# Sends in making order, k and v packed 5 and 4, q in quarters one block earlier, and a silu moved behind a copy

## The chip, the core and the metric

The kernel runs on one core of a Trainium2 chip. A core has TensorE (PE: matmuls, with its weight loads shown apart as PEld), VectorE (DVE), ScalarE (ACT), GpSimd (POOL) and SyncE (SP), which here does nothing but issue DMAs; its queue is called SPq. They run side by side and wait for each other through semaphores. Matmuls read SBUF and write into PSUM banks; VectorE and ScalarE carry the results from there into SBUF. GpSimd works on SBUF alone.

The metric is the device time of one execution in microseconds. The kernel before takes 1059.37 us (median of 3 runs, 1058.65 to 1060.12). The profile is of one execution with a span of 1058.9 us.

## The reference

Attention without softmax, with an RMS norm, and behind it a feed-forward block with a gate:

```python
# q, k, v: (8, 8, 576, 64) float32 = batch, head, position, dim; g_norm: (64,)
kv = np.einsum('bhsd,bhse->bhde', k, v)            # k^T v, 64 x 64 for each head
out = np.einsum('bhsd,bhde->bhse', q, kv)
rms = np.sqrt(np.mean(out * out, axis=-1, keepdims=True) + 1e-06)
attn = out / rms * g_norm

x = attn.transpose(0, 2, 1, 3).reshape(4608, 512)  # tokens x model
g = x @ w_gate                                     # w_gate, w_val: 512 x 1536
silu = g * (1.0 / (1.0 + np.exp(-g)))
val = x @ w_val
result = silu * val @ w_out                        # w_out: 1536 x 512
```

## The kernel before

The 4608 tokens go in nine blocks (n = 0 to 8) of 512. The attention of block n + 1 is worked into the feed-forward of block n. A feed-forward has an *up* part (w_gate and w_val, the silu, the product) and a *down* part (w_out).

Both parts use a Winograd form of Strassen's scheme: a product of 2 x 2 blocks in seven products instead of eight. They are called P1 to P7 and run in the order 1, 5, (4, 3 of the unit before), 6, 2, 7. Several of them add up in one PSUM bank, and intermediate states are copied out, so a product may only be added to a bank once the copy of the state before is done:

```python
    CHAIN = {1: ("b", True), 6: ("b", False), 7: ("b", False), 4: ("b", False), 2: ("a", True),
             5: ("c", True), 3: ("c", False)}          # bank of each product; True: a new one
    ...
    class Up(Quad):                                    # one of six units of the up part of block 1
        def sequence(self, last):
            return [(self, 1), (self, 5), (last, 4), (last, 3), (self, 6), (self, 2), (self, 7)]

        def after2(self):
            add(nc.vector, self.s, self.ps["a"], self.s)
            nc.scalar.activation(out=self.s, in_=self.s, func=ACT.Silu)

        def after7(self):
            self.u3 = self.piece(2)
            nc.scalar.copy(out=self.u3, in_=self.ps["b"])
            add(nc.vector, self.u3, self.ps["c"], self.u3)

        def after4(self):
            g = self.piece(3)
            nc.scalar.activation(out=g, in_=self.ps["b"], func=ACT.Silu)
            mul(nc.gpsimd, self.h[:, :, HB:BLK], g, self.u3)

        def after3(self):
            add(nc.vector, self.u2, self.ps["c"], self.u2)
            mul(nc.gpsimd, self.h[:, :, 0:HB], self.s, self.u2)
            self.ffn.ended = self.ffn.h_sums(self.j, 1, nc.vector)
```

Block 0 multiplies plainly, block 1 uses one level of the scheme (class `Up`), and blocks 2 to 8 use two in the up part (class `Inner`). The second level needs sums of sums of the weights. There are too many of these for SBUF, so block 1 makes them once on VectorE (`leaf_steps`), three steps after each product, and sends them to DRAM; the blocks after it read them back as a stream of 17 chunks for each of three d, through a pool of nine tiles (`t`). The same nine tiles hold the sums of weights that GpSimd makes for the first level. Each of the six j of block 1 sends when the steps of a group are done, ordered by chunk:

```python
        def send():
            for c, ops in enumerate(CHUNKS):
                dst = stream.dram[d, c]                # one DRAM tile for each chunk
                places = [at.get(op) for op in ops]
                if len(ops) == 2 and None not in places and places[0][0] is places[1][0]:
                    (src, i), (_, k) = places
                    tc.keep_in_program_order(nc.sync.dma_start(out=dst[:, :, f], in_=src[:, i : k + 1 : k - i]))
                    continue
                for m, place in enumerate(places):
                    if place:
                        tc.keep_in_program_order(nc.sync.dma_start(out=dst[:, m, f], in_=place[0][:, place[1]]))
```

k and v are loaded by pairs of heads (four j). The 576 positions of a head are nine groups of 64: five groups lie in partitions 0 to 63 and four in 64 to 127, so a tile of 1024 columns holds one j in 640 of them, and one quarter of those is empty in the lower half. The pool `ld` has four such tiles, shared by k, v, q and, at the start, the weights:

```python
        def kv(self, js):
            ...
            for j in js:
                for c in range(KT):                    # KT = 5
                    for r in range(2 if c < KT - 1 else 1):
                        rows = slice(r * D, (r + 1) * D)
                        for u in range(2):
                            nc.tensor.matmul(          # 64 x 64, 72 of them a block
                                self.kv_ps[r][u * D : (u + 1) * D, j, :], lhsT=self.k[j][rows, u, c, :],
                                rhs=self.v[j][rows, u, c, :], start=(c == 0), stop=(c == KT - 1 - r),
                            )
```

q must be turned. Up to block 3 TensorE does it, with 16 transposes of 128 x 128 and a copy out of PSUM. From block 4 on (`TURNED = 4`) q is loaded in 32 x 32 quarters by some 32 small DMAs, so that VectorE's transpose of 32 x 32 squares does the rest. In those blocks k and v come one j at a time, in four steps within the up part, since q takes two of the four tiles; before them two j at a time, in two steps:

```python
            elif n + 1 < TURNED:
                steps = {4: third, 8: two_thirds}      # after 4 and 8 twelfths of the up part
            else:
                steps = {3 * j + 2: lambda j=j: pair(j) for j in range(NS)}
```

Of the kernel before, what the change touches and what calls it, by code (L numbers as in the profile page):

```python
# [8 lines left out]
F32 = mybir.dt.float32  # L9
# [9 lines left out]
def kernel(  # L19
# [54 lines left out]
    KT = 5  # L74
    eps = 1e-6
# [42 lines left out]
    class Words:  # L118
# [12 lines left out]
        def __init__(self, src, shape):  # L131
            self.raw = ld_pool.tile([P, 2 * BLK], U32, name="ld")
            dst = self.raw.rearrange("p (a b) -> p a b", a=shape[0])
            nc.sync.dma_start(out=dst, in_=src)
            self.shape = shape
# [48 lines left out]
    class Att:  # L184


        def __init__(self, n):
            self.n = n

            self.cut, half = divmod(n, 2)  # L190
            self.split = half * D
            self.ps, self.z = {}, None
            self.q, self.k, self.v, self.room = [], [], [], None
            self.halves = []
# [10 lines left out]
        def place_kv(self, j, i):  # L205

            n = (2 * j + i) * 2 * KT * D
            if self.n == 0:
                return self.room.rearrange("p f t -> p (f t)")[:, n:]
            if self.n == 1 and j < 2:  # L210
                return self.room[:, n:]
            return ld_pool.tile([P, 2 * BLK], F32, name="ld")

        def load_kv(self, js):
            if self.n == B:
                return
            for j in js:
                hs = slice(2 * j, 2 * j + 2)
                for i, (tiles, src) in enumerate(((self.k, k), (self.v, v))):
                    t = self.place_kv(j, i)[:, 0 : 2 * KT * D].rearrange("p (h x) -> p h x", h=2)  # L220

                    for r, s0, m in ((0, 0, KT), (1, KT * D, KT - 1)):
                        nc.sync.dma_start(  # L223
                            out=t[r * D : (r + 1) * D, :, 0 : m * D],
                            in_=src[self.n, hs, s0 : s0 + m * D].rearrange("h (p t) d -> p h (t d)", t=m),
                        )
                    tiles.append(t.rearrange("p h (t d) -> p h t d", t=KT))

        def load_quarters(self, i):


            ld = ld_pool.tile([P, 2 * BLK], F32, name="ld")
# [16 lines left out]
        def load_q(self, i):  # L249
# [5 lines left out]
            else:  # L255
                ld = ld_pool.tile([P, 2 * BLK], F32, name="ld")
# [9 lines left out]
        def kv(self, js):  # L266
# [4 lines left out]
            if js[0] == 0:  # L271
                self.kv_ps = [m_psum.tile([P, NS, D], F32, name="m") for _ in range(2)]
            for j in js:
                for c in range(KT):
                    for r in range(2 if c < KT - 1 else 1):
                        rows = slice(r * D, (r + 1) * D)
                        for u in range(2):
                            nc.tensor.matmul(  # L278
                                self.kv_ps[r][u * D : (u + 1) * D, j, :], lhsT=self.k[j][rows, u, c, :],
                                rhs=self.v[j][rows, u, c, :], start=(c == 0), stop=(c == KT - 1 - r),  # L280
                            )
            if js[-1] == NS - 1:
# [111 lines left out]
        def first(self):  # L394
            self.turn_q(0, (b_psum, c_psum))
            self.kv(range(NS))
# [40 lines left out]
    TURNED = 4  # L437
# [44 lines left out]
    class Up(Quad):  # L482
# [22 lines left out]
        def after2(self):  # L505
            add(nc.vector, self.s, self.ps["a"], self.s)
            nc.scalar.activation(out=self.s, in_=self.s, func=ACT.Silu)

        def after7(self):
            self.u3 = self.piece(2)  # L510
            nc.scalar.copy(out=self.u3, in_=self.ps["b"])
            add(nc.vector, self.u3, self.ps["c"], self.u3)
# [145 lines left out]

    CHUNKS = (
# [5 lines left out]
    class Stream:  # L665


        def __init__(self):
            self.dram = {}
            for d in range(NP // 2):  # L670
                for c in range(len(CHUNKS)):
                    self.dram[d, c] = dram.tile([P, 2, 2, P], F32, name=f"w{d}_{c}")
            self.at = {op: (c, i) for c, ops in enumerate(CHUNKS) for i, op in enumerate(ops)}
# [7 lines left out]
        def pump(self):  # L681

            while self.next and not self.held[-9]:
                n, d, c = key = self.next.pop(0)
                k = len(CHUNKS[c])
                self.tiles[key] = t_tile(key).rearrange("p l (f c) -> p l f c", f=2)
                self.uses[key] = 2 * k
                nc.sync.dma_start(out=self.tiles[key][:, 0:k], in_=self.dram[d, c][:, 0:k])
# [19 lines left out]
    def leaf_steps(j, sources, room):  # L708
# [3 lines left out]
        at = {}  # L712
        i = 0
        for t, os in sources:
# [8 lines left out]
            )  # L723
            yield lambda b11=b11, t2_=t2_, to=to: sub(nc.vector, to[:, :, 1], b11, t2_)
            for m, o in enumerate(os):
                for r, p in enumerate((4, 7, 5)):
                    at[o, p] = room, i + 3 * m + r
                if o not in RESIDENT:
                    quarters = t[:, m].rearrange("p i e c -> p (i e) c")
                    for r, p in enumerate((1, 6, 2, 3)):  # L730
                        at[o, p] = quarters, r
            i += 3 * n

        def send():
            for c, ops in enumerate(CHUNKS):
                dst = stream.dram[d, c]
                places = [at.get(op) for op in ops]
                if len(ops) == 2 and None not in places and places[0][0] is places[1][0]:
                    (src, i), (_, k) = places
                    tc.keep_in_program_order(nc.sync.dma_start(out=dst[:, :, f], in_=src[:, i : k + 1 : k - i]))  # L740
                    continue
                for m, place in enumerate(places):
                    if place:
                        tc.keep_in_program_order(nc.sync.dma_start(out=dst[:, m, f], in_=place[0][:, place[1]]))

        yield send
# [88 lines left out]
    class Ffn:  # L835
# [22 lines left out]
        def up(self, fill):  # L858
# [11 lines left out]
            for i, this in enumerate(units):  # L870
                if i + 1 < len(units):
                    units[i + 1].prepare()
                for unit, p in this.sequence(last):
                    if unit:
                        unit.multiply(p)
                        self.make(3)
# [8 lines left out]
        def down(self, nxt):  # L885
# [3 lines left out]
            for p in (1, 5, 6, 7, 2, 4, 3):  # L889
# [5 lines left out]
                self.make(12)  # L895
# [151 lines left out]
```

## Time and profile before

| What | Value |
|---|---|
| Time | 1059.37 us (1058.65 to 1060.12) |
| VectorE busy | 701.7 us (66%) |
| ScalarE busy | 234.9 us (22%) |
| GpSimd busy | 367.5 us (35%) |
| DMA | 161.87 MB, q1 at 52.1% of 16 engines |
| Reads of the stream (`t<-w`) | 336 of 256 KB, 2.9 us each to landing, and 21 of 128 KB |
| Sends (`w<-t`, `w<-r`, `w<-xi`) | 36 + 6 + 18 of 128 KB, 42 + 36 of 64 KB, 1.8 to 2.2 us each to landing |

How to read it. A group is called by its source line, engine and tiles, output first: `t<-w` reads the stream from DRAM into a t tile, and `w<-t`, `w<-r` and `w<-xi` send parts of it. Sums, differences and products are recorded by small helpers, so L110 is any sum, L111 any difference and L112 any product. L460 is a matmul of `Quad` (`Up` and the down part), L609 one of `Inner`, L278 one of k^T v and L299 a transpose of q. L507 is the silu in `after2` and L511 the copy in `after7`; L740 and L744 are the sends, L688 the reads of the stream, L223 the loads of k and v and L241 those of q in quarters. A matmul of 32-bit numbers appears as two records. An entry such as [5.23 <-ACT r L511] says how long the engine had been idle and what released it.

### The profile page before, as it was taken

To read this page: it belongs to the slowest core of one execution; us is meant where nothing else is said; L and a number is where in the kernel's file an instruction comes from. 1 tells how busy PE (TensorE), PEld (TensorE's weight loads), DVE (VectorE), ACT (ScalarE), POOL (GpSimd) and SP (SyncE) were. 2 spreads that over 40 slices of the span, in tenths; PEclk is the share of its full clock that TensorE was granted. 3 is DMA by queue.
4 is the path that set the end of the run, shared out by engine and by line. 5 is a ranking of instruction groups with operands and counts; after the bars stand their busy time and mean duration, and the time that the engine had idled before them with its cause. 6 is when DMAs were issued, how large, how long until landed. Compare 5 with 4: busy or idle time off the path is not lost.

```text
span 1058.9 us, 21788 instructions
## 1 busy us (share of the span) xinstructions
PE 1032.9 (98%) x8700; PEld 928.2 (88%) x8700; DVE 701.7 (66%) x1255; ACT 234.9 (22%) x372; POOL 367.5 (35%) x280
## 2 busy tenths in 40 slices
PE   5899999998999999999999999999999999999998
PEld 5644688876899989998999899989999899989997
DVE  2999596777656766575666756676668556855661
ACT  2666211221112211111121211221111121112110
POOL 0000453344015711563056305640455126512670
PEclk9999999998999999999999999999999999999999
DMA  9887203565568436753476347643763266226601
GB/s 239 228 265 231 57 2 109 167 167 156 174 195 235 122 90 189 227 153 86 152 224 191 88 127 226 198 93 120 218 214 89 81 204 190 61 80 195 199 31 40
DMA packets 177076, 161.87 MB, mean 153 GB/s; under 512 B 70864, under 2 KB 128080, under 8 KB 176976
## 3 DMA queue, kind: packets, MB, share of 16 engines
q1 hardware_dynamic: 176912, 160.49, 52.1%
q8 instruction: 69, 1.13, 0.4%
q14 instruction: 31, 0.25, 0.1%
q0 software_dynamic: 64, 0.00, 0.0%
HBM read 138.02 MB, written 22.41 MB: 152 GB/s over the span
## 4 chain that ended last, share of the span: by engine, by line
PE 92%; DVE 3%; DMA 2%; SPq 2%; POOL 1%; issue 0%; ACT 0%; DVEq 0%; POOLq 0%; ACTq 0%
PE b L609 25%; PE b L460 20%; PE c L609 12%; PE c L460 10%; PE a L609 6%; PE a L460 5%; PE c L912 4%; PE b L912 4%; PE m L278 2%; PE m L366 1%; PE m L319 1%; SPq L223 1%; PE b L319 1%; DMA ld<-in_moe_w_gate_dram 1%; DVE r L111 1%; DVE r L110 1%
## 5 line engine op out<-in xcount | busy, mean ns | idle before, releaser
L110 POOL TENSOR_TENSOR r<-r 128x256 f32<-128x256 f32 (+1 forms) x105 | 110.4, 1056 | 343.4 <-DVE r L110 337.7
L110 DVE TENSOR_TENSOR r<-b,r 128x512 f32<-128x512 f32 (+1 forms) x273 | 162.2, 606 | 67.1 <-PE b L609 61.9
L111 POOL TENSOR_TENSOR t<-wo 128x512 f32<-128x512 f32 x81 | 113.5, 1422 | 185.6 <-DVE wo L110 107.7
L110 DVE TENSOR_TENSOR r<-c,r 128x512 f32<-128x512 f32 (+1 forms) x179 | 108.8, 618 | 94.7 <-PE c L609 51.6
L609 PE MATMUL b<-x,t 128*128 128x128 f32 x1092 | 151.5, 276 | 0.0
L609 PEld LDWEIGHTS b<-x,t 128*128 128x128 f32 x1092 | 136.3, 192 | 1.0
L110 DVE TENSOR_TENSOR r<-a,r 128x512 f32<-128x512 f32 (+1 forms) x99 | 62.5, 631 | 81.2 <-PE a L609 51.2
L609 PE MATMUL c<-xi,t 128*128 128x128 f32 x840 | 112.1, 275 | 0.0
L112 POOL TENSOR_TENSOR h<-r 128x1024 f32<-128x1024 f32 (+1 forms) x40 | 81.4, 2052 | 84.9 <-DVE r L110 71.4
L609 PEld LDWEIGHTS c<-xi,t 128*128 128x128 f32 x840 | 102.8, 192 | 0.0
L460 PE MATMUL b<-wo,h 128*128 128x256 f32 x432 | 98.2, 380 | 0.0
L460 PE MATMUL b<-t,h 128*128 128x256 f32 x432 | 97.1, 381 | 0.0
L460 PEld LDWEIGHTS b<-wo,h 128*128 128x128 f32 x432 | 80.6, 190 | 12.0 <-DVE h L112 1.8
L460 PEld LDWEIGHTS b<-t,h 128*128 128x128 f32 x432 | 80.7, 190 | 11.1 <-issue 0.2
L623 ACT COPY r<-b 128x512 f32<-128x512 f32 x63 | 36.9, 586 | 238.0 <-PE b L609 231.2
L609 PE MATMUL b<-xi,t 128*128 128x128 f32 x588 | 79.7, 276 | 0.0
L609 PEld LDWEIGHTS b<-xi,t 128*128 128x128 f32 x588 | 72.4, 192 | 0.0
L609 PE MATMUL b<-x,wg 128*128 128x128 f32 x336 | 52.3, 278 | 0.0
L609 PE MATMUL b<-x,wv 128*128 128x128 f32 x336 | 51.6, 276 | 0.0
L460 PE MATMUL c<-t,s 128*128 128x256 f32 x216 | 48.9, 383 | 0.0
L460 PE MATMUL a<-wo,h 128*128 128x256 f32 x216 | 48.3, 379 | 0.0
L460 PE MATMUL c<-wo,h 128*128 128x256 f32 x216 | 48.1, 379 | 0.0
(130 smaller groups left out, 1623.4 us busy)
## 6 DMA issues: line engine op xcount, KB each, us to landing
t<-w SPq DMA_DIRECT2D x336, 256.0 KB, 2.9
out_dram<-r SPq DMA_DIRECT2D x17, 512.0 KB, 2.9
ld<-in_moe_w_gate_dram SPq DMA_DIRECT2D x12, 512.0 KB, 4.9
ld<-in_moe_w_val_dram SPq DMA_DIRECT2D x12, 512.0 KB, 4.9
ld<-in_moe_w_out_dram SPq DMA_DIRECT2D x12, 512.0 KB, 4.3
w<-t SPq DMA_DIRECT2D x36, 128.0 KB, 2.1
ld<-in_k_dram SPq DMA_DIRECT2D x26, 160.0 KB, 3.3
ld<-in_v_dram SPq DMA_DIRECT2D x26, 160.0 KB, 3.4
```

The costliest lines, as they stand in the source:

```text
L110: add = lambda e, o, a, b: e.tensor_tensor(out=o, in0=a, in1=b, op=OP.add)
L111: sub = lambda e, o, a, b: e.tensor_tensor(out=o, in0=a, in1=b, op=OP.subtract)
L112: mul = lambda e, o, a, b: e.tensor_tensor(out=o, in0=a, in1=b, op=OP.mult)
L223: nc.sync.dma_start(out=t[r * D : (r + 1) * D, :, 0 : m * D], in_=src[self.n, hs, s0 : s0 + m * D].rearrange("h (p t) d -> p h (t d)", t=m),)
L278: nc.tensor.matmul(self.kv_ps[r][u * D : (u + 1) * D, j, :], lhsT=self.k[j][rows, u, c, :], rhs=self.v[j][rows, u, c, :], start=(c == 0), ...
L319: nc.tensor.matmul(self.ps[i][u][p : p + D, t, j, :], lhsT=self.qt[rows, 2 * i + t, j, p : p + D], rhs=kvs[b % 3][rows, j, :], start=True, ...
L366: nc.tensor.transpose(ps[:, e, t], xt[:, t, j + e], ident)
L460: nc.tensor.matmul(banks[e][:, e], lhsT=lhsT, rhs=rhs, start=first and i == 0 and (e == 0 or banks[0] is not banks[1]), stop=i == self.ste ...
L609: nc.tensor.matmul(ps[:, i, f], lhsT=self.weight(o, p, f), rhs=self.operand(o, p), start=first and (i, f) == (0, 0), stop=True, skip_group ...
L623: nc.scalar.copy(out=dst, in_=ps)
L912: nc.tensor.matmul(t, lhsT=w[f // 2][:, i, P * (f % 2) : P * (f % 2 + 1)], rhs=x[:, i, of], start=(i == 0), stop=(i == NS - 1),)
```

## The change

It has five parts.

- The stream lies in DRAM in the order in which it is made, one tensor for each d; a send carries all that a step has made, as soon as it is there. A read then takes two places of that tensor, which lie next to each other in seven of the seventeen chunks; one chunk is a single place and nine are two places apart. Block 1 does four making steps after each product, not three.
- k and v of two j share a tile: five groups of one j and four of the next in each half, 1152 columns without a gap. All of k and v of a block takes two steps.
- q comes in quarters from block 3 on (`TURNED = 3`), and those loads are moved from the start of the down part to behind its P5.
- The silu of `after2` goes behind the copy of P7.
- The ld tiles grow from 1024 to 1152 columns.

```diff
-    TURNED = 4
+    TURNED = 3
...
         def after2(self):
             add(nc.vector, self.s, self.ps["a"], self.s)
-            nc.scalar.activation(out=self.s, in_=self.s, func=ACT.Silu)

         def after7(self):
             self.u3 = self.piece(2)
             nc.scalar.copy(out=self.u3, in_=self.ps["b"])
+            nc.scalar.activation(out=self.s, in_=self.s, func=ACT.Silu)
             add(nc.vector, self.u3, self.ps["c"], self.u3)
...
+    LEAVES = [(o, p) for o in (5, 7, 4) for p in (1, 6, 2, 3)]
+    LEAVES += [(o, p) for os in ((5,), (7,), (4,), (1, 2), (6, 3)) for o in os for p in (4, 7, 5)]
...
-                nc.sync.dma_start(out=self.tiles[key][:, 0:k], in_=self.dram[d, c][:, 0:k])
+                nc.sync.dma_start(out=self.tiles[key][:, 0:count], in_=self.dram[d][:, i : k + 1 : max(k - i, 1)])
...
+        def send(leaf, count, src):
+            at = LEAVES.index(leaf)
+            tc.keep_in_program_order(nc.sync.dma_start(out=stream.dram[d][:, at : at + count, f], in_=src))
...                                                    # in leaf_steps, after the third step of a product
+            if os[0] not in RESIDENT:
+                yield lambda t=t, o=os[0]: send((o, 1), 4, t[:, 0].rearrange("p i e c -> p (i e) c"))
             yield lambda b11=b11, t2_=t2_, to=to: sub(nc.vector, to[:, :, 1], b11, t2_)
...
+            yield lambda i=i, n=n, o=os[0]: send((o, 4), 3 * n, room[:, i : i + 3 * n])
...
-                        self.make(3)
+                        self.make(4)
...                                                    # k and v: two j (e = 0, 1) in a tile
+            for e in range(2):
+                j = 2 * g + e
                 for c in range(KT):
-                    for r in range(2 if c < KT - 1 else 1):
-                        rows = slice(r * D, (r + 1) * D)
-                        for u in range(2):
+                    for r in range(2):
+                        m = KT - (r != e)
+                        for u in range(2 if c < m else 0):
                             nc.tensor.matmul(
-                                self.kv_ps[r][u * D : (u + 1) * D, j, :], lhsT=self.k[j][rows, u, c, :],
-                                rhs=self.v[j][rows, u, c, :], start=(c == 0), stop=(c == KT - 1 - r),
+                                self.kv_ps[r][u * D : (u + 1) * D, j, :], lhsT=self.k[j, r][:, u, c, :],
+                                rhs=self.v[j, r][:, u, c, :], start=(c == 0), stop=(c == m - 1),
                             )
...                                                    # in the down part
                 self.make(12)
+                if p == 5:
+                    for i in range(2):
+                        self.loads(i)
...
-            elif n + 1 < TURNED:
-                steps = {4: third, 8: two_thirds}
-            else:
-                steps = {3 * j + 2: lambda j=j: pair(j) for j in range(NS)}
-            ffn.up(steps)
+            ffn.up({4: third, 8: two_thirds} if nxt else {})
```

## The prediction

> **What bounds the kernel now.** I read the page first (busy time by engine), then the waits of TensorE, then the windows of the single blocks, and last the timeline of the one block in which TensorE stands still.
>
> ```profile
> PE 1032.9 (98%) x8700; PEld 928.2 (88%) x8700; DVE 701.7 (66%) x1255; ACT 234.9 (22%) x372; POOL 367.5 (35%) x280
> ```
>
> TensorE is busy 1032.9 of 1058.9 us, so at most 26 us can come from idle time; more needs fewer or better packed matmuls. The windows, one for each block of 512 tokens from block 2 on, show where it is full (columns: stretch, its length, then busy time of PE, PEld, DVE, ACT, POOL, granted clock, DMA share, GB/s):
>
> ```profile
> 295.00:407.00 112.00, 112.00 (x1065) 106.45 (x1064) 71.41 (x120) 22.65 (x35) 42.71 (x32) 1.00 0.57 162
> 407.00:517.70 110.70, 110.70 (x1046) 104.59 (x1046) 71.91 (x122) 20.60 (x31) 42.94 (x32) 1.00 0.55 159
> ...
> 849.80:956.90 107.10, 107.08 (x902) 101.67 (x902) 71.27 (x121) 20.34 (x30) 42.81 (x32) 1.00 0.45 132
> ...
> 162.34:250.52 88.18, 80.64 (x498) 69.50 (x497) 64.50 (x146) 17.86 (x32) 30.91 (x23) 0.96 0.53 146
> ```
>
> Blocks 2 to 7 have no gap: there only TensorE's own work counts. The last line is the up part of block 1, the only block that makes the streamed weights: 7.54 us idle, and the clock drops to 0.96. The waits of 160 to 300 us (waiter <- waited for: us in total, times, longest) name the links:
>
> ```profile
> ACT r L507 <- DVE r L110: 32.6, 6, 7.5
> ...
> POOL t L111 <- DMA w<-t: 13.1, 5, 4.6
> ...
> DVE s L110 <- POOL h L112: 12.1, 5, 2.9
> ...
> PE b L460 <- ACT r L511: 7.5, 2, 5.2
> ```
>
> and the timeline shows the second stall as one chain:
>
> ```profile
> 234.17 0.52 SPq L740 DMA_DIRECT2D w<-t  x1
> ...
> 234.68 1.27 POOL L111 TENSOR_TENSOR t<-wo 128x512 f32<-128x512 f32 x1 [1.21 <-DMA w<-t]
> ...
> 235.90 1.27 POOL L112 TENSOR_TENSOR h<-r 128x512 f32<-128x512 f32 x1
> ...
> 237.21 0.42 DVE L110 TENSOR_TENSOR s<-h 128x256 f32<-128x256 f32 x1 [2.93 <-POOL h L112]
> ...
> 241.19 0.68 DVE L110 TENSOR_TENSOR r<-a,r 128x512 f32<-128x512 f32 x1
> ...
> 241.91 0.63 ACT L507 ACTIVATE r<-r 128x512 f32<-128x512 f32 x1 [7.47 <-DVE r L110]
> ...
> 242.45 0.57 ACT L511 COPY r<-b 128x512 f32<-128x512 f32 x1
> ...
> 243.16 3.75 PE L460 MATMUL b<-x,t 128*128 128x256 f32 x8 [5.23 <-ACT r L511]
> ...
> 246.70 2.72 PE L460 MATMUL c<-x,wv 128*128 128x256 f32 x8
> ```
>
> GpSimd cannot refill a t tile before a send of its old content is done; VectorE waits for GpSimd's product; the sum of P2 comes late; ScalarE stands at the silu of that sum, with the copy of P7 behind it; and P4 may not add into that bank before the copy. The sends lag since the DMA queue is nearly full: the program has 138 of them (36 + 42 + 36 + 18 + 6 in the DMA view), and adding up that queue's timeline from 160 to 276 us gives 81.3 us for them and 94.9 us in all: 0.59 us a send.
>
> **What the Trainium skill says.** Perfetto Trace Analysis, section What "DMA-bound" means, counts as one kind of bound a DMA sequencer whose track is solid issue slices. It fits: 94.9 of 116 us, while the 16 DMA engines are only 0.53 busy. TensorE: Matmul & The Clock Gate, section What's actually happening, says that an idle window of some 3.4 us halves the clock. The trace agrees: after the 5.23 us gap four matmuls take 3.54 us (243.16 to 246.70) instead of 1.73, and the next four 2.56; the gap of 2.31 us slows nothing. DMA: Bandwidth & Descriptors, section Specifications, puts full rate at 512 B and more. I take the measured side: from 50 to 60 us the weight loads, in runs of 1 KB, keep the engines at a share of 1.01 with 296 GB/s, while the stream in runs of 2 KB has 159 GB/s at 0.55, which is 289 at a full share. So reads in runs of 1 KB should cost what they cost now.
>
> **The change part by part.**
>
> 1. *Sends by making order.* The sends of a j go from 23 to 8 (three products with two each, two pairs with one each), 138 to 48 in all: 48 x 0.59 = 28 us of issue in place of 81. Each also leaves right after the step that makes its data, no longer after all steps of its group. With it, three steps for each product of block 1 become four: a j has 20 sums and 8 sends, 28 steps, which is 4 x 7 products, so the making keeps pace. Now it is 24 steps against 3 x 7 = 21, so a rest is done in the down part. The t tiles come free sooner, and GpSimd's wait of 13.1 us should nearly go.
>
> 2. *Silu behind the copy of P7.* The copy no longer stands behind a wait for VectorE. P4 is free as soon as P7 ends. What is left is P3, which needs VectorE's sum of P7 out of bank c, and P4 before it takes 1.73 us, so VectorE may be later by that much for nothing.
>
> Parts 1 and 2 hit the same loss: 2.31 + 5.23 = 7.54 us idle, and the cold clock after it, (3.54 - 1.73) + (2.56 - 1.73) = 2.64 us; 10.2 us together. I keep 1.5 us of it as a rest, since VectorE gets tighter: 64.5 us busy now, and the making left after 250.5 us (seven sums in the timeline, 1.69 + 1.48 + 1.01 + 1.02 = 5.2 us) moves in, 69.7 us in about 78, 89%. Gain 8.7 us.
>
> 3. *q in quarters from block 3 on.* Block 3's q is turned on TensorE in block 2. Timeline of TensorE there:
>
> ```profile
> 360.37 0.60 PE L299 MATMUL m<-ident,ld 128*128 128x128 f32 x4
> ...
> 362.11 2.11 PE L460 MATMUL b<-wo,h 128*128 128x256 f32 x9
> ```
>
> 362.11 - 360.37 = 1.74 us leave TensorE. In return VectorE makes two 128x1024 transposes of 1.23 us (as the ten that it makes for later blocks), in a block where it is busy 71 of 112 us: free. The 32 small loads take 16.6 us of the DMA queue (361.43 to 378.06, for block 4 today). They now go into the down part, ahead of the first stream reads, as they already do in later blocks. Gain 1.7 us.
>
> 4. *k and v packed, two steps.* No matmul is saved: 72 of 64x64 a block, before and after. But each switch to 64x64 and back costs time. A burst of 36 (72 records in the timeline) runs from 311.73 to 313.04; the 18 of the quartered form (36 records) run from 430.67 to 431.39. The first is 1.31 us, the second 0.72 us, so two of 18 cost 0.13 us more than one of 36 in the burst alone. Around each, the matmul before and the group after it are drawn out by 0.10 us each (0.55 between the first and second group after, otherwise 0.45). So a burst of 36 costs 1.51 and two of 18 cost 1.84. For a block, 3.68 - 3.02 = 0.66 us. A cross-check: block 2 has two bursts and the transposes, block 3 four bursts and none, and chain starts give 111.76 (295.23 to 406.99) against 110.70; 111.76 - 1.74 = 110.02, which is 0.68 under 110.70. I take 0.68, for blocks 3 to 6: gain 2.7 us.
>
> 5. *Start.* The same 16 k and v loads in block 0, but all k of a pair of j ahead of its v, so the last matmuls wait for one load more. Cost 0.3 us by judgement; the wait for the gate weights behind it covers some.
>
> Sum: 8.7 + 1.7 + 2.7 - 0.3 = 12.8 us. From 1059.37 that is 1046.6 us.
>
> **Rivals.** *VectorE takes the stall over.* If it stays as late as now (its sum of P7 starts at 243.73, though P7 ended at about 237.1), P3 would wait where P4 waited: P4 at 237.9, done at 239.7, P3 not before 244.4 (243.73 + 0.68), so only 0.5 of the 5.23 us is won, and by the same reckoning 0.9 of the 2.31. That is 1.4 us instead of 8.7: about 1054 us. Against it: VectorE's lag in that chain is waiting (2.93 us and then 1.15 us for GpSimd), not work, and what GpSimd waited for is the send. *The stream starves.* All reads come from one tensor for each d, nine of the seventeen chunks (the strided pairs) in runs of 1 KB instead of 2, and 32 q loads stand before the first reads. If 1 KB runs halved the rate, the share of 0.55 would go towards 0.85, with TensorE waiting in every block, 1065 us or more. Against it: the 296 GB/s above, the nine t tiles of lead, and the first reads, which today start 15 us before their use (276.21 against 291.56) and need to start no later relative to it. *k and v loads hold up the queue.* A load that waits for k^T v blocks the reads behind it; today that is 26.0 us in 14 waits without one gap on TensorE, and block 2, which already loads in two steps, has none either. It would cost 0 to 4 us. *Only part 2 or only part 1 works*: either alone should remove most of the second stall, so the sum changes by 2 to 4 us.
>
> **Range and chances.** The 4.4 us of parts 3 and 4 are TensorE's own work, which nothing hides; I trust them to 1 us. The block 1 term can be 4 to 11 us. That gives 1043.5 to 1051. 2% is 21.2 us: faster than 1038.2 would need nearly all of the idle time of the kernel, of which some 15 us lie in the first 40 us that the change hardly touches: 2%. Slower than 1080.6 needs the starving stream in every block: 2%.
>
> **What would show it.** Right: no TensorE wait on ScalarE's copy in block 1; a granted clock of 1.00 there and an up part of 78 to 80 us; GpSimd's wait for sends under 4 us; 48 sends; blocks 2 to 6 at 110.0 us each; two k^T v bursts per block; no idle TensorE in blocks 2 to 7. Wrong: TensorE waiting for VectorE at the P3 of block 1 (first rival), or for stream reads in blocks 2 to 8, or a DMA share well above 0.55 at the same GB/s (second rival).

## The result, and the profile after

| | Before | After |
|---|---|---|
| Time, median | 1059.6 us (1058.65 to 1060.12, 4 runs) | 1053.33 us (1053.17 to 1053.51, 4 runs) |
| Ratio | 1 | 0.9942, 95% interval 0.9925 to 0.9959 |
| Span of the profiled execution | 1058.9 us | 1051.5 us |

Predicted were 1046.6 us, and 1043.5 to 1051 as the range. The kernel gained about half of the 12.8 us.

In the kernel after, the helpers are one line further down: L111 is any sum, L112 any difference, L113 any product. L468 is a matmul of `Quad`, L518 the copy of P7, L519 the silu of the sum of P2, L726 the sends. Busy time by engine, from the page:

```profile
PE 1026.1 (98%) x8684; PEld 923.0 (88%) x8684; DVE 706.9 (67%) x1257; ACT 232.7 (22%) x368; POOL 368.7 (35%) x280
```

The windows of the kernel after: the up part of block 1, then the blocks 2, 3, 6 and 7, each from its first P1 to that of the next block (columns as before):

```profile
162.45:247.60 85.15, 80.01 (x498) 68.89 (x497) 70.69 (x148) 17.67 (x32) 30.84 (x23) 0.98 0.63 175
...
292.45:402.43 109.98, 109.96 (x1047) 104.22 (x1046) 71.71 (x122) 20.69 (x31) 42.79 (x32) 1.00 0.56 160
402.43:512.41 109.98, 109.96 (x1046) 104.23 (x1046) 71.71 (x122) 20.69 (x31) 42.80 (x32) 1.00 0.56 160
...
732.37:842.35 109.98, 109.96 (x1046) 104.22 (x1046) 71.70 (x122) 20.69 (x31) 42.80 (x32) 1.00 0.52 149
842.35:949.42 107.07, 107.05 (x902) 101.69 (x901) 71.30 (x121) 20.32 (x30) 42.80 (x32) 1.00 0.44 132
```

Blocks 2 to 6 take 109.98 us each, full to the last 0.02, as predicted. The up part of block 1 takes 85.15 us with 5.14 of them idle; predicted were 78 to 80. Laid from one down chain's first matmul to the next, the profiled executions differ by: start +0.27; block 1 129.21 to 126.18, -3.03; block 2 111.76 to 108.84, -2.92; block 3 109.65 to 109.98, +0.33; blocks 4 to 6 110.70 to 109.98, three times -0.72; block 7 +0.06. That is 7.45 us; the spans differ by 7.4, the medians by 6.0 to 6.3, so the profiled execution of before was one of its longer ones. Block 1 alone falls short.

The waits of the kernel after from 160 to 300 us show that every link of the old chain is still there (waiter <- waited for: us in total, times, longest):

```profile
POOL t L112 <- DMA w<-t: 35.8, 6, 10.0
ACT r L519 <- DVE r L111: 33.3, 6, 7.5
...
DVE h L112 <- POOL h L113: 6.0, 3, 2.7
...
PE b L468 <- ACT r L518: 5.1, 4, 2.3
...
DVE s L111 <- POOL h L113: 2.3, 2, 1.2
```

and the timeline of one of the four stalls is the same chain as before, only shorter:

```profile
195.80 1.26 POOL L112 TENSOR_TENSOR t<-wg,wv 128x512 f32<-128x512 f32 x1 [3.03 <-DMA w<-t]
...
197.02 1.27 POOL L113 TENSOR_TENSOR h<-r 128x512 f32<-128x512 f32 x1
...
198.32 1.47 DVE L112 TENSOR_TENSOR h<-s,h 128x256 f32<-128x256 f32 x1 [2.74 <-POOL h L113]
...
200.84 0.68 DVE L111 TENSOR_TENSOR r<-a,r 128x512 f32<-128x512 f32 x1
...
201.56 0.63 ACT L519 ACTIVATE r<-r 128x512 f32<-128x512 f32 x1 [7.47 <-DVE r L111]
...
202.09 0.57 ACT L518 COPY r<-b 128x512 f32<-128x512 f32 x1
...
202.71 1.99 PE L468 MATMUL b<-x,t 128*128 128x256 f32 x8 [2.34 <-ACT r L518]
```

Three things are to be seen. The silu (L519) still runs ahead of the copy (L518): the scheduler that orders each engine's queue put it there, although the source now has it behind. GpSimd's product still stands behind a t tile that waits for a send. And the VectorE instruction at 198.32 lasts 1.47 us, while others of its form last 0.42.

The sends themselves are what the change promised, by the DMA view (KB each, median us to landing):

```profile
w<-t SPq DMA_DIRECT2D x18, 256.0 KB, 2.3
w<-xi SPq DMA_DIRECT2D x12, 384.0 KB, 3.0
...
w<-r SPq DMA_DIRECT2D x18, 192.0 KB, 2.2
```

48 of them, 21.0 us of issue by the queue's timeline from 160 to 276 us, against some 80 before. But the queue's own waits now show what it stands for:

```profile
SPq L726 <- DVE t L111: 22.4, 12, 5.4
SPq L726 <- DVE wg L112: 18.6, 5, 4.4
...
SPq L726 <- DVE s L111: 6.1, 4, 2.6
```

The queue is no longer full; most of what it waits for is VectorE's sums. But the loads of the next block still stand ahead of some sends. The t tile of 195.80 above waited for a send whose data VectorE had finished at 189.39 us. It left at 191.58, behind three loads of q:

```profile
189.10 0.29 DVE L111 TENSOR_TENSOR t<-t 128x128 f32<-128x128 f32 x1
...
189.34 2.13 SPq L267 DMA_DIRECT2D ld<-in_q_dram  x3
...
191.58 0.84 SPq L726 DMA_DIRECT2D w<-t  x1
```

By the trace it landed at 195.64, 4.06 us after its issue, against a median of 2.3. Before the stall at 231.43 it is the same with loads of k and v: the data were there at 219.23, the send left at 222.48 and landed at 225.41, just ahead of GpSimd's next t tile at 225.56. These are the two long stalls, 2.34 and 1.99 of 5.14 us. No run moves these loads, so their share stays open.

### VectorE is shut out while GpSimd works

The timeline of VectorE and GpSimd in the kernel after, at 190 us:

```profile
190.23 1.27 POOL L112 TENSOR_TENSOR t<-wg,wv 128x512 f32<-128x512 f32 x1 [5.85 <-DMA w<-t]
190.29 1.36 DVE L111 TENSOR_TENSOR t<-t 128x128 f32<-128x128 f32 x1
191.46 1.31 POOL L113 TENSOR_TENSOR h<-r 128x512 f32<-128x512 f32 x1
191.68 1.58 DVE L112 TENSOR_TENSOR r<-t 128x256 f32<-128x256 f32 x2
```

The sum at 190.29 takes 1.36 us in place of 0.28: it begins just after GpSimd's difference, which ends at 191.50, and ends 0.15 us behind it. In the up part of block 1, 19 VectorE sums and differences begin while a GpSimd instruction runs and have both inputs in SBUF. Two of them, begun within 15 ns of GpSimd's start, take their usual 0.28 us. The other 17 end a fixed time after GpSimd's end: 146 to 150 ns with 128 elements a partition, 279 to 284 with 256, 547 to 550 with 512. They do not run slower beside GpSimd; they stand still until it is done. Sums with an input in PSUM begin 303 times in the whole trace while GpSimd works, and take what they take elsewhere: medians of 415 ns (256 elements) and 691 ns (512).

The Trainium skill has this: SBUF — State Buffer, section SBUF: two separate sides, says that VectorE and GpSimd share a pair of ports under an exclusive lock: of a VectorE instruction with two SBUF inputs and a GpSimd instruction that reads SBUF, the one that starts first gets the pair for its whole length, and the other fully blocks. The 17 agree, with the numbers above; for the two that began within 15 ns the trace does not tell which had the ports.

The trace counts the time shut out as busy. I add up, over the VectorE sums, differences and products of the up part of block 1 that a GpSimd instruction overlaps, the time above the shortest of the same form, and call it *shut-out time*: 10.9 us before, 16.9 us after (of 78.7 us, all durations added). In the kernel before, it was hidden in VectorE's 64.5 us of busy time.

### The profile page after: what moved, and what is told of

The parts are those of the page before. It is cut to its first block, busy times and chain, and to the rows that moved or that the text cites. A ratio compares the mean times of both kernels' runs of the same rounds, so it can differ in the third digit from the quotient of the medians.

```text
span 1051.5 us, 21628 instructions
## 1 busy us (share of the span) xinstructions
PE 1026.1 (98%) x8684; PEld 923.0 (88%) x8684; DVE 706.9 (67%) x1257; ACT 232.7 (22%) x368; POOL 368.7 (35%) x280
## 4 chain that ended last, share of the span: by engine, by line
PE 91%; DVE 4%; DMA 2%; SPq 2%; issue 1%; ACT 0%; POOL 0%; DVEq 0%; ACTq 0%; POOLq 0%
PE b L617 25%; PE b L468 20%; PE c L617 12%; PE c L468 10%; PE a L617 6%; PE a L468 5%; PE c L911 4%; PE b L911 4%; PE m L285 2%; PE m L373 1%; PE m L326 1%; SPq L228 1%; PE b L326 1%; DMA ld<-in_moe_w_gate_dram 1%; DVE xi L112 1%
## 5 line engine op out<-in xcount | busy, mean ns | idle before, releaser
L111 POOL TENSOR_TENSOR r<-r 128x256 f32<-128x256 f32 (+1 forms) x105 | 110.1, 1055 | 326.9 <-DVE r L111 276.2
L111 DVE TENSOR_TENSOR r<-b,r 128x512 f32<-128x512 f32 (+1 forms) x273 | 161.9, 606 | 61.8 <-PE b L617 57.2
L112 POOL TENSOR_TENSOR t<-wo 128x512 f32<-128x512 f32 x81 | 115.7, 1452 | 187.1 <-DVE wo L111 109.3
L111 DVE TENSOR_TENSOR r<-c,r 128x512 f32<-128x512 f32 (+1 forms) x179 | 108.7, 617 | 96.5 <-PE c L617 53.6
L111 DVE TENSOR_TENSOR r<-a,r 128x512 f32<-128x512 f32 (+1 forms) x99 | 62.5, 631 | 80.9 <-PE a L617 50.9
L113 POOL TENSOR_TENSOR h<-r 128x1024 f32<-128x1024 f32 (+1 forms) x40 | 81.6, 2054 | 90.7 <-DVE r L111 76.9
L468 PE MATMUL b<-wo,h 128*128 128x256 f32 x432 | 98.8, 381 | 0.1
L468 PE MATMUL b<-t,h 128*128 128x256 f32 x432 | 97.1, 382 | 0.0
L468 PEld LDWEIGHTS b<-wo,h 128*128 128x128 f32 x432 | 80.6, 190 | 12.5 <-DVE h L113 2.5
L468 PEld LDWEIGHTS b<-t,h 128*128 128x128 f32 x432 | 80.8, 190 | 10.9 <-issue 0.2
L468 PE MATMUL c<-t,s 128*128 128x256 f32 x216 | 48.9, 383 | 0.0
L338 DVE TENSOR_REDUCE z<-r 128x8 f32<-128x512 f32 x36 | 23.0, 678 | 37.9 <-ACT r L337 37.8
L468 PE MATMUL a<-wo,h 128*128 128x256 f32 x216 | 48.3, 379 | 0.0
```

The source lines that it names most:

```text
L111: add = lambda e, o, a, b: e.tensor_tensor(out=o, in0=a, in1=b, op=OP.add)
L112: sub = lambda e, o, a, b: e.tensor_tensor(out=o, in0=a, in1=b, op=OP.subtract)
L113: mul = lambda e, o, a, b: e.tensor_tensor(out=o, in0=a, in1=b, op=OP.mult)
L338: nc.vector.tensor_reduce(out=self.z[:, i, u], in_=sq, axis=mybir.AxisListType.X, op=OP.add)
L468: nc.tensor.matmul(banks[e][:, e], lhsT=lhsT, rhs=rhs, start=first and i == 0 and (e == 0 or banks[0] is not banks[1]), stop=i == self.ste ...
```

## The experiments

Two theories came out of this. *C*: VectorE is full in block 1, its own work plus what GpSimd shuts out. *Q*: VectorE has the time, but waits in its queue for GpSimd's products, which wait behind t tiles for sends. The texts of E1 to E4 are older and use other letters: A is the order on ScalarE; B is VectorE's lateness, in E2 put down to its waits for GpSimd; "rival C" there is a late GpSimd and not the C of here; S and D are for and against the sends.

A table of all runs (down chain: start of the first matmul of block 1's down part; PE waits: TensorE's for ScalarE's copy and VectorE's c sum in the up part; shut out: in the up part; for h: VectorE's waits for GpSimd's products from 162 to 255 us):

| Run | Time, us | Ratio to before, 95% | Down chain | PE waits | Shut out | For h |
|---|---|---|---|---|---|---|
| before | 1059.6 | 1 | 250.35 | 7.5 | 10.9 | 17.5 |
| after | 1053.33 | 0.9925 to 0.9959 | 247.59 | 5.1 | 16.9 | 8.3 |
| E1 copy first | 1052.74 | 0.9923 to 0.9952 | 247.06 | 4.1 | 19.3 | 5.9 |
| E2 h sums on GpSimd | 1055.35 | 0.9947 to 0.9977 | 248.75 | 6.5 | 24.0 | 0 |
| E3 both | 1053.97 | 0.9934 to 0.9964 | 247.23 | 6.1 | 25.3 | 0 |
| E4 old sends | 1059.3 | 0.9985 to 1.0002 | 254.67 | 8.8 | 12.5 | 14.2 |
| E5 make three | 1052.35 | 0.9921 to 0.9948 | 245.07 | 4.0 | 21.5 | 3.3 |
| E6 products first | 1056.25 | 0.9954 to 0.9977 | 249.28 | 6.9 | 25.6 | 1.8 |
| E7 products on VectorE | 1047.84 | 0.9878 to 0.9905 | 241.89 | 1.8 | 10.8 | 0 |
| E8 h sums later | 1050.50 | 0.9901 to 0.9928 | 244.99 | 3.7 | 23.6 | 0.6 |
| E9 = E7, silu first | 1048.98 | 0.9885 to 0.9915 | 244.06 | 2.5 | 10.9 | 0 |
| E10 = E7 + E8 | 1046.28 | 0.9863 to 0.9890 | 240.34 | 0.6 | 12.0 | 0 |
| E11 = E7, old sends | 1057.67 | 0.9981 to 0.9996 | 249.10 | 6.2 | 10.7 | 0 |
| E12 part 1 alone | 1057.39 | 0.9973 to 0.9986 | 248.10 | 5.7 | 21.3 | 3.2 |

The last two columns together are what VectorE loses to GpSimd. They add up to 24.0 to 28.4 us in all ten kernels with the products on GpSimd, and to 10.7 to 12.0 in the four that have them on VectorE. Where the waits for h go, shut-out time comes in their place.

**E1, the order that part 2 meant.** The kernel after, with the silu held behind the copy in ScalarE's queue:

```diff
-            nc.scalar.copy(out=self.u3, in_=self.ps["b"])
-            nc.scalar.activation(out=self.s, in_=self.s, func=ACT.Silu)
+            copied = nc.scalar.copy(out=self.u3, in_=self.ps["b"])
+            with tc.issue_after(copied.ins):
+                nc.scalar.activation(out=self.s, in_=self.s, func=ACT.Silu)
```

> The changed kernel with the silu really queued behind the copy of P7 on ScalarE (in the changed kernel's trace the silu still stands ahead of it). Theory A, the order on ScalarE is the link that stalls TensorE: no TensorE wait on that copy is left; P4 goes on at once and only P3 may wait for VectorE's sum out of bank c. Read off the changed trace the stalls then shrink by 1.0, 0.5 and 2.7 us (the last with its cold clock) and 0.3: up part of block 1 about 81 us instead of 85.15, time about 1049 us. Theory B, VectorE's lateness is the cause and the order on ScalarE does not matter: P3 waits where P4 waited, up part 84 us or more, time 1052 to 1053.5 us.

1052.74 us (1052.56 to 1052.84). P4 no longer waits for the copy at 202 us; P3 behind it waits instead, by TensorE's timeline of E1, and in the next line VectorE's c sum is what it waits for:

```profile
203.57 1.99 PE L468 MATMUL c<-x,wv 128*128 128x256 f32 x8 [1.37 <-DVE r L111]
```

```profile
202.83 0.68 DVE L111 TENSOR_TENSOR r<-c,r 128x512 f32<-128x512 f32 x1
```

So the wait moved to the place that the first rival named, as theory B has it, and part 2, when it is really there, brings 0.6 us.

**E2 and E3, the sums of h to GpSimd.** VectorE's work and its waits for h are both cut; E3 adds E1's order.

```diff
-            self.ffn.ended = self.ffn.h_sums(self.j, 1, nc.vector)
+            self.ffn.ended = self.ffn.h_sums(self.j, 1, nc.gpsimd)
```

> The changed kernel with the two sums of h in each unit of block 1 on GpSimd instead of VectorE; the order on ScalarE stays silu, copy. Theory B, VectorE is late because it waits in its queue for GpSimd's product of h and back: these waits go (6.0 + 2.3 us in all), the sum of P2 comes 2 to 3 us sooner, stalls on the copy fall under 1 us, up part 79 to 81 us, time about 1048 us. Theory A alone: the silu still waits for VectorE's own work, so half of the stall stays, up part 82 to 83 us, time about 1051 us. Rival C, GpSimd becomes late with 12 more sums: t tiles or h come late and TensorE waits for GpSimd, up part 85 us or more.

> Both: copy ahead of the silu, and the sums of h on GpSimd. Theories A and B: no stall on ScalarE or VectorE in block 1, up part 78 to 79 us at a clock of 1.00, time about 1046.5 us, which is what was predicted for the change. Rival C: TensorE waits for GpSimd, no better than with the copy first alone.

1055.35 us (1054.47 to 1055.99) and 1053.97 us (1052.96 to 1054.85): slower than the same kernels without it, by 2.0 and 1.2 us. VectorE lost twelve sums of 0.42 us, 5.0 us of work, and every wait for h; but its shut-out time rose by 7.1 us in E2 (16.9 to 24.0) and 6.0 in E3 (19.3 to 25.3). Waits for the send of the xi tile (4.2 and 3.0 us) are new on VectorE too. Work taken from VectorE came back mostly as time in which VectorE was shut out. The time is that of the texts' rival C, but its picture is not: TensorE waits for the copy (4.9 us in E2) and for VectorE's c sum (1.5 and 6.1 us), and no gap of its matmuls in the up part ends with GpSimd. That speaks for C.

**E4, the sends as before.** The kernel after with the chunk tensors and sends of before, and three making steps:

```diff
-            self.dram = [dram.tile([P, len(LEAVES), 2, P], F32, name=f"w{d}") for d in range(NP // 2)]
+                    self.dram[d, c] = dram.tile([P, 2, 2, P], F32, name=f"w{d}_{c}")
...                        # and send() by chunk at the end of a group, as before
-                        self.make(4)
+                        self.make(3)
```

> The changed kernel with the stream's sends and reads as before (138 sends by chunk, three making steps after a product); all other parts of the change kept. Theory S, the new sends gave the 2.8 us that block 1 gained: its up part is back at 88 us, time about 1056.3 us, with 138 sends filling the DMA queue. Rival D, the sends do not limit (GpSimd's wait for them is longer in the changed kernel, 35.8 against 13.1 us): up part 85 us, time about 1053.3 us. Blocks 2 to 6 stay at 109.98 us in either case.

1059.3 us (1056.86 to 1060.39): all 6.0 us of the change are gone, twice what theory S had put on the sends. Blocks 3 to 6 keep 109.97 to 110.10 us, so parts 3 and 4 are still there; their gain is lost again ahead of them, where block 1's down chain begins 4.3 us later than before (1.3 of them at the start, the rest in block 1).

**E5, less making in the up part** (E1 with one more line changed; C and Q differ in sign):

```diff
-                        self.make(4)
+                        self.make(3)
```

> The changed kernel with ScalarE's copy ahead of its silu (as in the copy-first run, 1052.7 us), and three steps of making after each product in place of four; the rest of the making falls into the down part. Theory C (VectorE is full in the up part of block 1: its own work, drawn out beside GpSimd's): about 18 sums less there, some 6 us of VectorE's work; the 4.1 us in which TensorE waits for VectorE's c sum fall under 1.5 us and the time to 1050 to 1051 us. Theory Q (the chain send, t tile, GpSimd's product, VectorE's sum of h): the sends leave later, GpSimd waits longer for t tiles than 33 us, and the time is 1053 us or more.

1052.35 us (1050.88 to 1053.14), not to be told from E1's. Its premise failed: the up part lost 6 VectorE instructions (148 to 142), not 18, and VectorE stayed 73.3 us busy. Inconclusive.

**E6, GpSimd's products ahead of its t tiles** (E1, with the t tiles of the next unit behind the second product):

```diff
-                if i + 1 < len(units):
+                if i + 1 < len(units) and last is None:
                     units[i + 1].prepare()
...
+                    if unit and p == 3 and i + 1 < len(units) and self.n < DEEP:
+                        with tc.issue_after(unit.product.ins):
+                            units[i + 1].prepare()
```

> The copy-first kernel with GpSimd's two h products of a unit issued ahead of the three t tiles of the next, so that no product stands behind a wait for a send. VectorE's work is the same. Theory Q: VectorE's 5.9 us of waits for GpSimd's h go, its sums come 2 to 3 us sooner in the two late units, TensorE's 4.1 us of waits for the c sum fall under 1.5 us, 1050 to 1051 us. Theory C: the waits move, but VectorE stays full; the time stays within 0.7 us of 1052.7. A third outcome: the t tiles, now last on GpSimd, come too late for P5 of the next unit, and TensorE waits for them: over 1053.5 us.

1056.25 us (1054.18 to 1056.77), 3.5 us slower than E1. VectorE's waits for h fell from 5.9 to 1.8 us as Q asks, but its shut-out time rose from 19.3 to 25.6 us, and TensorE waits longer, 4.9 us at once, for VectorE's c sum. It is the time of the third outcome, but not its cause: its three stalls are all waits for VectorE's c sum (1.39, 0.64 and 4.87 us), none for a t tile. VectorE's timeline ahead of that stall, then GpSimd's:

```profile
222.99 1.64 DVE L112 TENSOR_TENSOR xi<-wv 128x512 f32<-128x512 f32 x1
224.55 1.48 DVE L112 TENSOR_TENSOR h<-s,h 128x256 f32<-128x256 f32 x1
225.96 1.49 DVE L112 TENSOR_TENSOR xi<-wv 128x256 f32<-128x256 f32 x1
227.36 1.49 DVE L112 TENSOR_TENSOR wg<-wg 128x256 f32<-128x256 f32 x1
228.89 1.37 DVE L111 TENSOR_TENSOR wg<-wg 128x256 f32<-128x256 f32 x1
230.18 0.68 DVE L111 TENSOR_TENSOR r<-a,r 128x512 f32<-128x512 f32 x1
```

```profile
222.70 1.38 POOL L113 TENSOR_TENSOR h<-r 128x512 f32<-128x512 f32 x1 [4.21 <-DMA ld<-in_k_dram]
224.04 1.71 POOL L112 TENSOR_TENSOR t<-wv 128x512 f32<-128x512 f32 x1
225.72 2.86 POOL L112 TENSOR_TENSOR t<-wg,wv 128x512 f32<-128x512 f32 x2
228.53 2.85 POOL L112 TENSOR_TENSOR t<-wo 128x512 f32<-128x512 f32 x2
```

GpSimd has its work in one run, and VectorE gets through one instruction for each of GpSimd's: five in 7.2 us that take 2.4 us by themselves (0.69 and four of 0.42). The a sum stands behind them. Q alone cannot explain this; C does.

**E7, the products on VectorE** (E1, and in `after4` and `after3`):

```diff
-            mul(nc.gpsimd, self.h[:, :, HB:BLK], g, self.u3)
+            mul(nc.vector, self.h[:, :, HB:BLK], g, self.u3)
...
-            mul(nc.gpsimd, self.h[:, :, 0:HB], self.s, self.u2)
+            mul(nc.vector, self.h[:, :, 0:HB], self.s, self.u2)
```

> The copy-first kernel with the twelve h products of block 1 on VectorE, not GpSimd. VectorE gets 12 x 0.68 = 8.2 us more work of its own. Theory C: each product of 1.27 us on GpSimd draws out a VectorE sum beside it by about 1.1 us, up to 13 us for twelve; without them the drawn-out time in the up part falls from 19.3 us to 8 to 11 us, VectorE's busy time is no longer, its 5.9 us of waits for h go: 1051 to 1052.5 us. If nothing is drawn out by GpSimd (theory Q without C), VectorE has 8.2 us more and 5.9 us less to wait: about 1053.5 to 1055 us.

1047.84 us (1047.49 to 1048.61), 4.9 us faster than E1 and better than either theory asked. The windows of the up part, first of E1, then of E7:

```profile
162.45:247.22 84.77, 80.53 (x499) 68.91 (x498) 72.96 (x148) 17.93 (x32) 30.66 (x23) 0.98 0.62 173
```

```profile
162.45:241.89 79.44, 77.55 (x495) 67.22 (x494) 70.76 (x159) 18.33 (x32) 17.12 (x12) 1.00 0.67 187
```

VectorE runs 11 instructions more and is busy 2.2 us less. The products cost it 12 x 0.68 = 8.2 us, its shut-out time falls by 8.5 us, and its 5.9 us of waits for h are gone: both theories' parts, in one edit. A GpSimd instruction of this shape can shut VectorE out for some 1.08 us (1.36 - 0.28 above), more than the 0.68 it takes VectorE to make the product. GpSimd also has 13.5 us less to do (30.66 to 17.12), but its t tiles come no sooner: it still waits 34.4 us for sends, and three q loads still stand ahead of one. TensorE no longer stalls behind that.

**E8, the sums of h behind the c sum** (E1, with no engine's work changed):

```diff
-            add(nc.vector, self.u3, self.ps["c"], self.u3)
+            summed = add(nc.vector, self.u3, self.ps["c"], self.u3)
+            if self.j:
+                with tc.issue_after(summed.ins):
+                    self.ffn.h_sums(self.j - 1, 1, nc.vector)
...
-            self.ffn.ended = self.ffn.h_sums(self.j, 1, nc.vector)
+            if self.j == NP - 1:
+                self.ffn.ended = self.ffn.h_sums(self.j, 1, nc.vector)
```

> The copy-first kernel with the two sums of h of a unit issued on VectorE behind the c sum of the next unit's P7, no longer ahead of its a and c sums. Work of every engine is the same. Theory Q: the a and c sums no longer stand behind a wait for GpSimd; TensorE's 4.1 us of waits for the c sum fall under 1.5 us, 1050 to 1051 us. Theory C: VectorE is as full as before, but 2 x 0.42 us of a unit, or up to 1.5 us where drawn out, now stand behind the c sum: at most half of the 4.1 us goes, 1051.5 to 1052.7 us.

1050.50 us (1049.76 to 1051.01), 2.2 us faster than E1, with waits for h at 0.6 us. The time is Q's, but 3.7 us of TensorE's waits stay, where Q allowed 1.5. So Q is a part of it: 2.2 of the 6.5 us that lie between E1 and the best version, E10. VectorE does not lose less to GpSimd here, 24.2 us against 25.2 (its shut-out time rose from 19.3 to 23.6); but the sums of h no longer stand ahead of the a and c sums. That suggests that only what is lost ahead of those two counts.

**E9, E7 without the enforced order** (the kernel after, with the two product lines of E7 only).

> The changed kernel with the twelve h products on VectorE and nothing else: ScalarE's queue stays silu first, copy of P7 second, as the scheduler leaves it. If the copy's place matters only when VectorE's a sum is late, TensorE now waits little for it: 1047.5 to 1049 us. If the place matters in itself, P4 waits for the copy in several units as in the changed kernel (5.1 us there): 1050 us or more.

1048.98 us (1048.4 to 1049.73), 1.1 us slower than E7. Three waits of TensorE for the copy are left, from its timeline:

```profile
215.58 1.99 PE L468 MATMUL b<-x,t 128*128 128x256 f32 x8 [0.59 <-ACT r L518]
...
228.26 1.99 PE L468 MATMUL b<-x,t 128*128 128x256 f32 x8 [0.33 <-ACT r L518]
239.44 1.97 PE L468 MATMUL b<-x,t 128*128 128x256 f32 x8 [1.62 <-ACT r L518]
```

Two lines that move twelve products bring 4.3 us by themselves; the copy's place is worth about 1.

**E10, E7 and E8 together.**

> The products-on-vector kernel (1047.8 us) with the two sums of h of a unit behind the c sum of the next unit's P7. There 1.8 us of TensorE's waits for the c sum are left (0.75 and 1.02 us). Theory C: VectorE's queue ahead of the a and c sums gets 0.84 us shorter, so at most half of the 1.8 us stays: 1046 to 1047.3 us. If the sums only move the load, no difference: 1047.8.

1046.28 us (1046.02 to 1046.81), the best version of this study: 13.1 us under its runs of before, 7.0 under the changed kernel. The window of its up part:

```profile
162.45:240.34 77.89, 77.21 (x496) 67.28 (x494) 71.43 (x157) 18.32 (x32) 16.00 (x12) 1.00 0.67 187
```

It is 10.3 us shorter than before (88.18), about the 10.2 us that the prediction had counted as lost there. 0.6 us of waits are left, and VectorE is still busy for 92% of it.

**E11, E7 with the old sends** (E7 and E4's edit).

> The products-on-vector kernel with the sends and chunk tensors of before (138 small sends, three steps of making after each product). If the sends act only through h products that stand behind waiting t tiles on GpSimd, they no longer matter: 1047.5 to 1049.5 us. If late t tiles also hold TensorE (its P5, P7, P4 read them), or VectorE's making is then held by sends from the shared xi tile, the 6 us that the new sends are worth in the changed kernel remain: 1052 to 1054 us.

1057.67 us (1056.81 to 1060.80). The old sends cost 9.8 us here, more than in E4. No product waits on GpSimd any more, so they act in another way too; from the waits of 162 to 258 us:

```profile
DVE xi L112 <- DMA w<-xi: 11.4, 7, 3.6
```

The old sends of a pair leave at the end of its group and wait in the queue, and VectorE may not write the shared xi tile before they are done; in E7 that wait is 1.9 us. A further 2.97 us gap of TensorE lies in the down part, at 269 us, where VectorE does the rest of the making.

**E12, part 1 on the kernel before** (its new tensors, sends and fourth making step; k, v, q and silu as before).

> The kernel before with part 1 alone: the 48 sends by making order, one tensor for each d, four steps of making. Old k and v loads, q and silu. If the parts add up, part 1 is worth what its removal from the changed kernel cost, 6.0 us: about 1053.5 us. If the changed kernel's loads of k, v and q are what crowd the queue of the old sends, part 1 alone is worth less, the 2.8 us by which the up part of block 1 got shorter: 1056 to 1057 us.

1057.39 us (1055.98 to 1058.44), 1.9 us under its runs of before. The parts do not add up: part 1 alone brings 1.9, parts 3 and 4 alone nothing (E4, in whose queue the silu stands first as in the kernel before), all together 6.0. Parts 3 and 4 keep their gain in blocks 2 to 6 in E4; what does not add up lies in block 1. What the old sends lose in block 1 beside the new loads is seen (GpSimd's waits for sends from 162 to 255 us are 11.5 us before, 23.7 in E4), but which load brings it was not tried and stays open.

## Why the prediction was wrong

**The failed step is the 8.7 us of parts 1 and 2**, the claim that VectorE will be on time once the sends are early. Block 1 gained 3.0 us in the profiled executions, and by the medians some 1.4 to 1.6 (6.0 to 6.3 less the 4.7 of parts 3 and 4). Two sentences in it failed. "The copy no longer stands behind a wait for VectorE" is false of the kernel as it runs: the silu kept its place in the queue. But that is worth only 0.6 us (E1).

The weightier one stands in the argument against the first rival: "VectorE's lag in that chain is waiting (2.93 us and then 1.15 us for GpSimd), not work, and what GpSimd waited for is the send." As a reading of the kernel before this is right: from 237.21 us to the c sum at 243.73 none of VectorE's instructions is drawn out. The step from it is wrong, that time no longer waited is time that VectorE has. When the waits for h shrink, from 17.5 to 8.3 us, more of VectorE's sums fall under GpSimd's instructions: shut-out time rises from 10.9 to 16.9 us and takes away much of the gain, and the profile counts it as busy. The sends, now issued as VectorE's sums end, are late with them.

Point by point:

- *Part 1, "GpSimd's wait of 13.1 us should nearly go"*: wrong. It rose to 35.8 us. A send now mostly waits for its sum, and ahead of the two long stalls for loads of q, k and v, so a shorter queue does not free a tile earlier. The total is no measure of the cost, either: it is 48.3 us in E9, at 1048.98 us. The 48 sends were right; at 0.44 us each (21.0 / 48) they are cheaper than the 0.59 assumed.
- *"89%" of VectorE in the up part* was the warning in the prediction's own sum. E10 reaches 92% without a stall to speak of, so the figure was possible, but only with the products off GpSimd and the sums in another order. The prediction took free time on an engine for time at the right moment.
- *The size of the prize was right.* With VectorE freed, the up part takes 79.44 us (E7) and 77.89 us (E10) at a clock of 1.00. The change did not hold the means to get there.
- *The first rival*, VectorE takes the stall over, was the true one: about 1054 us was written there, 1053.33 measured. Its picture, P3 waiting for the c sum, shows in E1. Its reason does not: it left VectorE's lag as it was, while in the run half of the waits for h went and shut-out time came in their place.
- *Parts 3 and 4*: right. 4.4 us predicted; by the chain starts of blocks 2 to 7 it is 2.92 - 0.33 + 3 x 0.72 - 0.06 = 4.69 us.
- *Part 5*: not to be told. 0.3 us was predicted and the start grew by 0.27 (121.14 to 121.41), but the twelve kernels with the new loads have this point anywhere from 120.50 to 122.43 us.
- *The stream starves; k and v hold up the queue*: neither, from block 2 on. Blocks 2 to 6 have 0.02 us idle each, at the DMA share of before (0.56), and a read of 256 KB takes 3.1 us to landing in place of 2.9, though in nine of the seventeen chunks its two places lie 3, 9 or 12 apart. In block 1 loads of q, k and v did hold up sends.

## What to carry to other kernels

Before counting on an engine's free time, compare the shortest and the longest instruction of one form on it: a VectorE sum that takes 0.28 us in most places and 1.36 in some is being shut out, and the busy share hides it. A small product handed to GpSimd is no gift to VectorE if VectorE sums SBUF tiles meanwhile. And read the order of each queue from what was built, not from the source: a line moved there need not move the instruction.

## What was not expected of the hardware

The shut-out hits single-input instructions too, if they are of a certain kind: in the kernel after, fifteen small `TENSOR_SCALAR` of 128x16, which take 0.175 us alone, take 1.15 to 1.19 when begun under a GpSimd instruction, while sixteen reductions of 128x512 take 0.68 either way.

The length of a gap does not decide by itself whether TensorE is slow after it. The first line, of the kernel after, follows a gap of 1.99 us; the second, of E5, one of 2.00 us:

```profile
231.43 2.80 PE L468 MATMUL b<-x,t 128*128 128x256 f32 x8 [1.99 <-ACT r L518]
```

```profile
242.15 1.99 PE L468 MATMUL c<-x,wv 128*128 128x256 f32 x8 [2.00 <-DVE r L111]
```

Both are groups of four matmuls of the same shape, two records each; they take 2.80 us in one case and 1.99 in the other. The granted clock tells why. In the kernel after it drops to half at 27.68 and at 232.48 us: 204.80 us apart, which is 60 steps of 3.413 us, and in all thirteen traces with more than one such drop, that at the end of the work counted, they lie whole steps apart. Windows of such a step, first of the kernel after, then of E5 (the columns are as before, the clock is the third from the end):

```profile
229.07:232.48 3.41, 1.42 (x7) 0.95 (x6) 3.38 (x10) 1.59 (x3) 0.00 (x0) 1.00 0.70 197
232.48:235.89 3.41, 3.41 (x10) 2.70 (x9) 2.48 (x10) 0.60 (x1) 0.95 (x1) 0.50 0.93 263
```

```profile
237.04:240.45 3.41, 3.00 (x16) 2.15 (x14) 3.38 (x9) 0.97 (x2) 0.04 (x1) 1.00 0.02 5
240.45:243.86 3.41, 1.71 (x8) 1.53 (x9) 3.34 (x7) 0.73 (x2) 1.27 (x1) 1.00 0.00 0
```

The first gap lies whole within one step, which leaves 1.99 us of it idle; the next step is at half clock. E5's gap falls on the border of two, with 0.4 and 1.7 us idle, and the clock stays. In all fourteen traces, from 110 to 1040 us, a step at full clock is followed by one at half clock if TensorE is idle in it for 1.935 us or more (nine steps), and never up to 1.926 us. So an idle time well under the 3.4 us of the prediction is enough, if it falls into one step. This is read off the traces; no run placed a gap on purpose.
